# Three weight pieces on another DMA queue, their conversions re-placed, 42 filler products, and four hand-written lists rewritten in a DeltaNet + MLP kernel

## The chip, the core and the metric

The kernel runs on one core of a Trainium2 chip. The metric is the device time of one execution in microseconds (us), as the median of several runs. Engines are named as in the profile: PE (TensorE's matrix products; PEld is its loading of the stationary operand), DVE (VectorE), ACT (ScalarE), POOL (GpSimd), SP (SyncE, which here only issues DMAs). "The clock" is the share of TensorE's full clock that the chip granted.

## What is computed

All tensors are fp32 on the device; the two weight matrices arrive as 64-bit floats and are read as pairs of 32-bit words.

```python
# attention part: q, k, v are (4, 8, 768, 48), beta is (4, 8, 768)
k_n = k / (norm(k, axis=-1) + 1e-6)
state = 0
for t in range(768):
    y[:, :, t] = einsum('bhd,bhde->bhe', q[:, :, t], state)
    v_old = einsum('bhde,bhd->bhe', state, k_n[:, :, t])
    state = state + beta[:, :, t] * einsum('bhd,bhe->bhde', k_n[:, :, t], v[:, :, t] - v_old)
x = y.transpose(0, 2, 1, 3).reshape(4, 768, 384)
# MLP part: w_ch1 (384, 1536), w_ch2 (1536, 384)
mu, var = mean(x, -1), mean((x - mu) ** 2, -1)
xn = (x - mu) / sqrt(var + 1e-6) * g_ln
out = x + maximum(xn @ w_ch1, 0) @ w_ch2
```

## The kernel before

**Tiling.** The 768 time steps are cut into 12 chunks of 64. Two chunks form a slab. A chunk holds all 32 pairs of batch and head, so one chunk is 256 tokens of the MLP. The recurrence inside a chunk is turned into matrix form: a Gram matrix of the keys (`gram`, "G"), the inverse of a unit triangular matrix made from it, the masked product of keys and queries (`product`, "PT"), and then `recur`, in seven steps: the products with the state ("KQ", line 640, followed on DVE by line 645), the solved values u ("U", lines 651 and 655), the state's update ("S", lines 663 and 666), the chunk's output y ("PU", lines 671 and 676), and the layer norm ("L1" lines 682 to 685, "L2" lines 687 to 690, "N" lines 698 and 699).

**The inverse.** It is worked out on DVE by columns, 31 columns of two instructions (lines 543 and 548) for a slab; a generator yields after each second column, so "one step" is four such DVE instructions. In front of the steps stand "ga" (a clearing multiplication on ACT, line 522, which needs the tile xb of the inverse before to be free, and the turning of the Gram matrices on DVE, line 460), "sq" (a square root on ACT, line 527) and "no" (DVE, lines 529 to 537). Behind them stand "own" (line 466, two transposes), "xt" (lines 451 and 455) and "xn" (line 559). A block of 32 is inverted this way, and `join` ("J", three pieces) puts two blocks together by products on PE (p_e, line 568; p_z, line 614), scaled copies on ACT (line 581) and copies on DVE and ACT (line 619). A prime at a name means the slab of the current chunk, no prime means the next slab. The first slab has blocks of 16 (`first_blocks`) and one more joining stage, `first_join` (lines 598 to 607).

**The MLP.** "H" is one of 12 hidden pieces: six PE instructions (line 732) and a ReLU on ACT (line 736), in two PSUM banks used by turns, so an H can start only when the ReLU of the H two before it has run. The second product is done with seven products of half size, P1 to P7 (line 787, twelve PE instructions each), sums of their operands on DVE, S1 to S4 and the four "T" that are made once (line 716), and seven result sums d1 to d7 (all in line 792). The first chunk's MLP (`ffn`) has the plain form.

**The weights.** They come in 12 pieces of 768 KB ("words", three buffers). `to_fp32` turns one piece into fp32 in five steps: one on ACT (line 300), four on DVE (lines 302, 304, 308 and 313). The next piece can be fetched when a buffer is free.

**Order.** There are three stretches. In the first (lines 836 to 909) the program's order is kept on every engine and queue (`in_this_order`): it prepares chunks 0 and 1 and carries chunk 0 through `recur`, with `keep_warm` products on a tile of zeros in between. In the second (lines 934 to 953) a `Plan` gives each piece a due time, and the tile framework sets the order. The third (lines 959 to 1041) goes by "slots", again with the order kept on every engine: slot c does `recur` of chunk c and the MLP of chunk c - 1, in the order of a list of names. Slots 2 to 5 have lists of their own in `orders`; slots 6 and on take `even` and `odd` by turns. Whatever a list doesn't name with "r" is done at "R": `left` counts the steps. TK and TQ turn the loaded keys and queries on DVE (line 336), Vk is the keys' norm (three squares on ACT, line 402 and 404, two sums on DVE, line 408, a root on ACT) and Vs scales v by it (line 418).

Of the kernel before, what the change touches and what calls it, by code (L numbers as in the profile page):

```python
# [82 lines left out]
def kernel(  # L83
# [127 lines left out]
    def fetch_words(eng=nc.gpsimd):  # L211
        if len(words) < len(pieces):
            src = pieces[len(words)][1]
            words.append(early_pool.tile([128, WN, 2], U32, name="words", bufs=3))
            out_ = words[-1].rearrange("p n w -> p (n w)")
# [338 lines left out]
    def join(chunks, both=()):  # L554
# [6 lines left out]
        for c, xn in zip(chunks, xns):  # L561
# [12 lines left out]
            for e in range(2):  # L574
                r1 = slice(e * C + BK, (e + 1) * C)
                if both and e:
                    for _ in both:
                        pass
                    nc.vector.tensor_scalar_mul(es[r1], p_e[r1], -1.0)
                else:  # L580
                    nc.scalar.mul(es[r1], p_e[r1], -1.0)  # L581
# [236 lines left out]
    NW = len(pieces)  # L818

# [16 lines left out]
    with in_this_order(tc) as last:  # L836
        grams_01 = []
        keep_warm(3)
        for c in two:
# [3 lines left out]
            next(grams_01[c])  # L843
        inv = first_blocks(two)
        for _ in range(3):
# [3 lines left out]
        for _ in range(3):  # L849
            fetch_words(nc.scalar)  # L850
# [3 lines left out]
        nc.vector.tensor_scalar_mul(scale_w[:, 1, 0:KC], g_sb, 2.0**-52)  # L854
        for i in range(FB // 2):
            next(inv)
            if i == 4:
                keep_warm(4, mark=True)
        knrm = norm_parts(0, xts[NXT - 1])
        next(knrm)  # L860
        joining = first_join(0)
        next(joining)
        keep_warm(1, 4)
        turned(0, 1)
        knrm = next(knrm)
        scale_v(0, knrm)
        piece = to_fp32(0)
        for _ in range(3):
            next(piece)
# [4 lines left out]
        joining = join((0,), both=piece)  # L874
        next(joining)
        next(joining)
        keep_warm(1)
        piece = to_fp32(1)
        next(piece)
# [5 lines left out]
        fetch_words()  # L885
# [12 lines left out]
        for _ in piece:  # L898
            pass
        fetch_words()  # L900
        piece = to_fp32(2)
        next(piece)
        for i in range(4):
            next(recur_0)
            if i == 1:
                keep_warm(4)
        for _ in piece:
# [40 lines left out]
    plan.spread(inverses[1], 3 + BK // 4, 24, 38, whole=False)  # L948
# [3 lines left out]
    with behind(tc, after):  # L952
# [7 lines left out]
        2: """O H H H H H H H H R' own' H KQ xt' xn' H J' T T T T H H J' P1 S1 U J' S2 d1 P2 d2 S S4 PU  # L960
            TK(a2) P6 d6 S3 L1 G(a2) P5 d5 TK(b2) L2 P7 d7 N G(b2) TQ(b) P3 d3 PT(b) P4 d4
            ga sq no Vk Vs""",
        3: """KQ H r H r H r H r U TQ(a2) H r H r H r S H r H r H H H PU P1 L1 S1 S2 d1 PT(a2) P2
# [108 lines left out]
```

## Time and profile before

| | |
|---|---|
| median of 13 runs | 577.27 us (573.87 to 581.63) |
| the profiled execution | 576.48 us, of which the span from the first to the last instruction is 574.6 us |
| busy share of the span | PE 92%, PEld 79%, DVE 69%, ACT 30%, POOL 3% |
| mean granted clock | 0.958 |
| first stretch | about 0 to 57 us |
| second stretch | about 57 to 120 us |
| start of KQ in slots 2 to 7 | 134.39, 174.11, 216.45, 259.40, 307.60, 345.57 us |

A timeline row gives the start in us, the duration in us, the engine, the line, the operation, the tile written and those read, the shapes (for PE rows x columns of the stationary operand, then out), and how many like instructions were merged. In brackets stand the engine's idle time before it and what ended it; "issue" means that nothing the profile shows was waited for. A window row gives, for each engine, the busy time and the number of instructions, then the granted clock, the DMA engines' busy share and GB/s. PE's fp32 products appear as two instructions each, and each of these as one weight load and one product.

### The profile page before, as it was taken

The numbers are of one execution on the slowest core, as the hardware profiler recorded it, in microseconds if no ns is written. First come the engines' busy times: TensorE is split into PE (matmuls) and PEld (weight loads), VectorE is DVE, ScalarE is ACT, GpSimd is POOL, SyncE is SP. The second block draws the span as 40 slices with busy tenths as digits, with TensorE's granted clock in tenths as the row PEclk, the third lists the DMA queues.
The fourth block names the chain that finished last, engine by engine and source line by source line (L and its number), as shares of the span: only waits on it lengthen the run. The fifth ranks groups of instructions, "written<-read, shape, count | busy, mean of one in ns | idle before, by whom it ended". The sixth has DMA issues, their size and how long they took to land.

```text
span 574.6 us, 20506 instructions
## 1 busy us (share of the span) xinstructions
PE 528.1 (92%) x9298; PEld 451.2 (79%) x9298; DVE 394.3 (69%) x815; ACT 173.2 (30%) x352; POOL 15.3 (3%) x36
## 2 busy tenths in 40 slices
PE   5389896987998999999999999999999999999996
PEld 2155675566887898798888898888898988988996
DVE  5866987999568998499974899736899540523212
ACT  1233344311353224512225322255222232222120
POOL 6000110000000000000000000000000000000000
PEclk9577997989899999999989999999999999999999
DMA  4646987760046235024324204203212010010101
GB/s 59 140 152 130 193 202 186 118 110 1 3 62 108 29 42 101 5 29 84 47 33 93 30 1 86 29 14 74 30 35 51 2 31 2 1 30 1 29 0 29
DMA packets 158390, 34.47 MB, mean 60 GB/s; under 512 B 153680, under 2 KB 156768, under 8 KB 158304
## 3 DMA queue, kind: packets, MB, share of 16 engines
q1 hardware_dynamic: 143776, 22.27, 24.0%
q0 software_dynamic: 1456, 7.10, 3.7%
q10 hardware_dynamic: 13072, 3.80, 2.9%
q8 instruction: 73, 1.20, 0.8%
q14 instruction: 13, 0.11, 0.1%
HBM read 28.43 MB, written 4.72 MB: 58 GB/s over the span
## 4 chain that ended last, share of the span: by engine, by line
PE 59%; DVE 16%; issue 12%; DMA 5%; ACT 4%; ACTq 2%; POOL 1%; SPq 0%; DVEq 0%; POOLq 0%
PE p_h L732 25%; PE p_a L787 12%; PE p_o L787 9%; DVE xb L548 3%; DVE tmp L543 3%; DMA words<-in_moe_w_ch_dram 2%; PE p_u L651 2%; PE p_e L568 2%; PE p_g L358 1%; DMA tb<-in_k_dram 1%; PE p_z L614 1%; PE p_g L383 1%; PE p_k L640 1%; PE p_s L663 1%; PE p_y L671 1%
## 5 line engine op out<-in xcount | busy, mean ns | idle before, releaser
L732 PE MATMUL p_h<-xnt,w_sb 128*128 128x256 f32 x864 | 201.5, 389 | 5.6 <-ACT h L736 2.6
L732 PEld LDWEIGHTS p_h<-xnt,w_sb 128*128 128x128 f32 x864 | 163.5, 193 | 30.8 <-ACT h L736 3.5
L736 ACT ACTIVATE h<-p_h 128x256 f32<-128x256 f32 x144 | 55.0, 383 | 154.7 <-PE p_h L732 147.9
L548 DVE TENSOR_TENSOR xb<-xb,tmp 128x31 f32<-128x31 f32 (+20 forms) x170 | 56.9, 335 | 5.7
L543 DVE TENSOR_TENSOR tmp<-xb,gb 128x31 f32<-128x31 f32 (+15 forms) x155 | 52.6, 339 | 4.2
L787 PE MATMUL p_o<-w_sb,h 128*128 128x192 f32 x264 | 48.0, 332 | 0.0
L787 PE MATMUL p_a<-t,h 128*128 128x192 f32 x264 | 47.0, 328 | 0.0
L787 PEld LDWEIGHTS p_o<-w_sb,h 128*128 128x128 f32 x264 | 42.7, 190 | 0.9
L787 PEld LDWEIGHTS p_a<-t,h 128*128 128x128 f32 x264 | 42.8, 190 | 0.3
L682 DVE BATCH_NORM_STATS2 st<-x_ln 128x6 f32<-128x384 f32 x24 | 12.9, 542 | 34.6 <-ACT x_ln L676 34.5
L830 PE MATMUL p_w<-zeros 128*64 128x512 f32 (+1 forms) x30 | 21.5, 862 | 14.0 <-DVE zeros L827 10.8
L787 PE MATMUL p_a<-t,s 128*128 128x192 f32 x132 | 25.2, 343 | 2.9 <-DVE o L792 2.8
L787 PEld LDWEIGHTS p_a<-t,s 128*128 128x128 f32 x132 | 23.1, 201 | 3.8 <-DVE o L792 3.7
L699 ACT COPY xnt<-p_n 128x384 f32<-128x384 f32 x24 | 10.4, 482 | 51.0 <-PE p_n L698 51.0
L619 DVE COPY xt<-p_z 32x512 f32<-32x512 f32 x12 | 8.1, 678 | 23.7 <-PE p_z L614 23.7
L787 PE MATMUL p_a<-w_sb,h 128*128 128x192 f32 x132 | 24.3, 334 | 0.0
L787 PE MATMUL p_o<-w_sb,s 128*128 128x192 f32 x132 | 23.6, 328 | 0.0
L830 PEld LDWEIGHTS p_w<-zeros 128*64 128x64 f32 x30 | 4.9, 187 | 22.3 <-DVE zeros L827 10.9
L787 PEld LDWEIGHTS p_o<-w_sb,s 128*128 128x128 f32 x132 | 21.6, 190 | 0.1
L787 PEld LDWEIGHTS p_a<-w_sb,h 128*128 128x128 f32 x132 | 21.2, 190 | 0.6
L358 PEld LDWEIGHTS p_g<-kt 48*64 48x64 f32 (+1 forms) x896 | 13.9, 132 | 9.6 <-issue 4.5
L581 ACT ACTIVATE es<-p_e 32x512 f32<-32x512 f32 x23 | 13.5, 589 | 25.8 <-PE p_e L568 25.5
(123 smaller groups left out, 691.3 us busy)
## 6 DMA issues: line engine op xcount, KB each, us to landing
words<-in_moe_w_ch_dram POOLq DMA_DIRECT2D x9, 768.0 KB, 5.9
out_dram<-o SPq DMA_DIRECT2D x48, 96.0 KB, 2.8
k<-in_k_dram SPq DMA_DIRECT2D x44, 96.0 KB, 3.0
v_raw<-in_v_dram SPq DMA_DIRECT2D x22, 192.0 KB, 4.3
tb<-in_k_dram SPq DMA_DIRECT2D x48, 64.0 KB, 2.5
tb<-in_q_dram SPq DMA_DIRECT2D x44, 64.0 KB, 2.8
words<-in_moe_w_ch_dram ACTq DMA_DIRECT2D x3, 768.0 KB, 7.3
tb<-in_q_dram SPq DMA_DIRECT2D x44, 32.0 KB, 2.8
```

Of the source, the lines that this page charges most:

```text
L358: nc.tensor.matmul(out_, kt[rows, i, r0 : r0 + (BK if fine else C)], kt[rows, i, r0:C])
L543: nc.vector.tensor_tensor(out=t, in0=xb[:, :, 0:n, j : j + 1].to_broadcast([128, nb, n, w]), in1=gb[:, :, j : j + 1, j + 1 : L].to_broadca ...
L548: nc.vector.tensor_tensor(out=rest, in0=rest, in1=t, op=ALU.subtract)
L568: nc.tensor.matmul(p_e[r1, h], gsb[r0, h, BK:C], xn[r0, h])
L581: nc.scalar.mul(es[r1], p_e[r1], -1.0)
L651: nc.tensor.matmul(p_u[half(e ^ hp), hp, j], xt[half(e), 2 * j + hp], vv[half(e), 2 * j + hp])
L682: nc.vector.bn_stats(out=st[:, g], in_=y[:, g])
L699: nc.scalar.copy(xnts[c][:, :, g * 128 : (g + 1) * 128], p_n)
L732: nc.tensor.matmul(p_h, w1_sb[:, t, f * 128 : (f + 1) * 128], xnt[:, t], start=(t == 0), stop=(t == KC - 1),)
L736: nc.scalar.activation(h[f // HF][:, f % HF], p_h, ACTF.Relu)
L787: nc.tensor.matmul(p[n], a[:, f], b[:, f], start=(first and f == 0), stop=(f == HF - 1), skip_group_check=True,)
L830: nc.tensor.matmul(p_w[0:64, 0:width], zeros, zeros[:, None, :].to_broadcast([128, width, 64]), start=True, stop=True,)
```

## The change

In the first stretch:

- The first three weight pieces are no longer issued from ACT's queue behind the loads of q, k and v of chunk 0, but from SP's queue, at three places of the inverse of the first slab. A DVE memset of one element of the buffer holds each back until DVE is there.
- 42 `keep_warm` products of 64 columns are put on PE behind the two Gram matrices; the one of 256 columns behind `first_join`'s first half goes.
- The steps of the conversions of pieces 0, 1 and 2 are put at other places of the first chunk's chain, and `scale_v` of chunk 0 is moved behind the scaled copies of `join`.

In the second stretch six steps of the inverse of slab 1 are planned instead of eight, due two units earlier; the other two fall to slot 2. In the third stretch the lists of slots 2 to 5 are rewritten; `even` and `odd` stay.

```diff
-    def fetch_words(eng=nc.gpsimd):
+    def fetch_words(eng=nc.gpsimd, held=False):
...
+            if held:
+                nc.vector.memset(words[-1][0:1, 0:1, 0].bitcast(FP32), 0.0)
...
-    def join(chunks, both=()):
+    def join(chunks, both=False):
...
                 if both and e:
-                    for _ in both:
-                        pass
                     nc.vector.tensor_scalar_mul(es[r1], p_e[r1], -1.0)
...
+    EARLY = 6
...
+        keep_warm(42, 1)
         inv = first_blocks(two)
-        for _ in range(3):
+        next(inv)
+        fetch_words(nc.sync, held=True)
+        for _ in range(2):
             next(inv)
         load_blocks(q, 0, 1, (nc.scalar,))
         load_kv(0, nc.scalar)
-        for _ in range(3):
-            fetch_words(nc.scalar)
         for gen in grams_01:
             next(gen, None)
...
+        knrm = norm_parts(0, xts[NXT - 1])
+        next(knrm)
+        parts = [to_fp32(i) for i in range(3)]
+        next(parts[0])
         for i in range(FB // 2):
             next(inv)
+            if i in (1, 4):
+                fetch_words(nc.sync, held=True)
             if i == 4:
                 keep_warm(4, mark=True)
-        knrm = norm_parts(0, xts[NXT - 1])
-        next(knrm)
         joining = first_join(0)
         next(joining)
-        keep_warm(1, 4)
+        next(parts[0])
         turned(0, 1)
+        next(parts[0])
         knrm = next(knrm)
-        scale_v(0, knrm)
-        piece = to_fp32(0)
-        for _ in range(3):
-            next(piece)
+        next(parts[1])
+        next(parts[0])
         next(joining)
         masking = product(0)
         next(masking)
         to_xt(0)
-        joining = join((0,), both=piece)
+        joining = join((0,), both=True)
         next(joining)
+        next(parts[0], None)
+        fetch_words()
         next(joining)
+        next(parts[2])
+        scale_v(0, knrm)
         keep_warm(1)
-        piece = to_fp32(1)
-        next(piece)
...
         keep_warm(1)
-        fetch_words()
...
         next(recur_0)
         next(recur_0)
         keep_warm(1)
-        for _ in piece:
-            pass
+        for _ in range(3):
+            next(parts[1])
+        next(recur_0)
+        next(parts[1], None)
         fetch_words()
-        piece = to_fp32(2)
-        next(piece)
-        for i in range(4):
-            next(recur_0)
-            if i == 1:
-                keep_warm(4)
-        for _ in piece:
+        next(recur_0)
+        keep_warm(4)
+        next(recur_0)
+        next(parts[2])
+        next(recur_0)
+        for _ in parts[2]:
             pass
         fetch_words()
...
-    plan.spread(inverses[1], 3 + BK // 4, 24, 38, whole=False)
+    plan.spread(inverses[1], 3 + EARLY, 24, 36, whole=False)
...
-        2: """O H H H H H H H H R' own' H KQ xt' xn' H J' T T T T H H J' P1 S1 U J' S2 d1 P2 d2 S S4 PU
-            TK(a2) P6 d6 S3 L1 G(a2) P5 d5 TK(b2) L2 P7 d7 N G(b2) TQ(b) P3 d3 PT(b) P4 d4
-            ga sq no Vk Vs""",
-        3: """KQ H r H r H r H r U TQ(a2) H r H r H r S H r H r H H H PU P1 L1 S1 S2 d1 PT(a2) P2
-            d2 L2 S4 P6 d6 S3 TK(a4) P5 d5 r N r P7 d7 G(a4) TK(b4) P3 d3 r G(b4) P4
-            d4 r Vk Vs""",
-        4: """KQ H H R' own' H H H xt' xn' H H H J' H J' U H J' ga S H TQ(b) H sq no PU P1 L1 S1
-            S2 d1 PT(b) P2 d2 L2 S4 P6 d6 S3 r P5 d5 r N r P7 d7 r P3 d3 r P4 d4 Vk
-            Vs""",
-        5: """KQ H r H r H r H r U r H r H r H r TQ(a2) S H R H H TK(a4) H own H PU P1 L1 S1 S2 d1
-            PT(a2) P2 d2 L2 S4 P6 xt d6 S3 P5 d5 xn N TK(b4) P7 d7 J G(a4) P3 d3 J
-            G(b4) P4 d4 J Vk Vs""",
+        2: """O H H H H H H H H H H H R' own' KQ H xt' xn' P1 J' T T d1 P2 S1 T J' T d2 S2 U J' S4
+            S PU P6 d6 S3 L1 TK(a2) P5 d5 L2 G(a2) TK(b2) P7 d7 N G(b2) Vk TQ(b) P3 d3 PT(b) P4
+            d4 Vs ga""",
+        3: """KQ H H sq H no H r H r U TQ(a2) H r H r H r S H r H r H H PU P1 L1 S1 S2 d1 PT(a2)
+            P2 d2 L2 S4 P6 d6 S3 TK(a4) P5 d5 r N r P7 d7 G(a4) TK(b4) P3 d3 r G(b4) P4 d4 r
+            Vk Vs""",
+        4: """KQ H H R' own' H H H xt' xn' ga H H sq H J' no H J' r U H J' r S H r TQ(b) H r PU P1
+            L1 S1 S2 d1 PT(b) P2 d2 L2 S4 P6 d6 S3 r P5 d5 r N r P7 d7 r P3 d3 r P4 d4 Vk Vs""",
+        5: """KQ H r H r H r H r H R U TQ(a2) H H own TK(a4) H S H H xt H xn H PU P1 L1 S1 S2 d1
+            PT(a2) P2 d2 L2 S4 P6 d6 S3 TK(b4) J P5 d5 G(a4) N P7 d7 J P3 d3 G(b4) J P4 d4
+            Vk Vs""",
...
-    left[1] -= BK // 4
+    left[1] -= EARLY
```

## The prediction

> **What bounds the kernel now.** I read the page first, then windows cut at the three stretches and the slots, then the timeline around each gap of PE.
>
> ```profile
> PE   5389896987998999999999999999999999999996
> ...
> PEclk9577997989899999999989999999999999999999
> ...
> q8 instruction: 73, 1.20, 0.8%
> ```
> ```profile
> 0.00:57.00 57.00, 37.72 (x933) 20.11 (x933) 38.25 (x90) 15.91 (x27) 9.78 (x28) 0.76 0.54 120
> 57.00:120.88 63.88, 53.20 (x1086) 38.49 (x1087) 56.71 (x98) 24.06 (x44) 5.49 (x8) 0.95 0.82 167
> 120.88:345.57 224.69, 213.36 (x3882) 189.85 (x3883) 179.12 (x383) 72.28 (x147) 0.00 (x0) 0.97 0.29 47
> 345.57:574.60 229.03, 223.82 (x3399) 202.72 (x3398) 120.19 (x247) 60.99 (x134) 0.00 (x0) 1.00 0.14 28
> ```
>
> The columns are the stretch, its length, busy us of PE, PEld, DVE, ACT and POOL, the clock, DMA share and GB/s. Before 57 us neither engine is full: a chain of handshakes for chunk 0. From 57 to 120.88 DVE is busy 56.7 of 63.9 us, so it sets the pace, and a shift of its start goes through to the end. In slots 2 to 6 PE has 11.3 us of idle, behind them almost none. The rewritten lists can win no more than these 11.3 us and what the half clock in them costs.
>
> **The first chunk.** This is the stall that the fillers answer to:
>
> ```profile
> 30.05 1.26 PE L598 MATMUL p_e<-x_n,gsb 32*32 32x16 f32 x128
> ...
> 31.90 0.83 PE L606 MATMUL p_z<-own,es 32*32 32x16 f32 x78
> ...
> 35.25 0.60 PE L606 MATMUL p_z<-own,es 32*32 32x16 f32 x50 [2.52 <-issue]
> ...
> 35.90 0.42 DVE L607 TENSOR_TENSOR own<-own,p_z 128x256 f32<-128x256 f32 x1 [1.99 <-PE p_z L606]
> ```
>
> PE stops in the middle of one matrix product and waits for nothing that is seen. Counting PE's pairs (load and product) from the start, the gap at 11.23 comes after 223 pairs, this one after 478: 255 apart. The next, 0.32 us at 38.28, comes 127 pairs on. The instruction queue's packets are 1.20 MB / 73 = 16 KB. So PE's instructions come in blocks of about 128 pairs, and while one runs, one is fetched; from 35.25 to 38.60 that took 3.35 us, from about 30.7 (within L598) to 35.25 it took 4.5 with the DMA engines loaded by the words.
>
> The 42 fillers are 84 pairs, and 2 pairs go: all later block ends fall 82 pairs earlier in the program. One then lies in the four marked warm products at 24 us, the next 2 or 3 pairs before the end of L598 (about 31.4), the next 3 pairs before the end of L606. L598 has its block in time; the one for L606's end is there at 31.4 + 3.35 to 4.5 = 34.75 to 35.9. p_z ended at 35.85, so the gain is 0 to 1.1; I take 1.0, as the words are off the DMA engines by then. The 0.32 at 38.28 goes too: 1.3.
>
> The Trainium skill, "Runtime: NRT & Kernel Launch", section "Instruction fetch mechanics", speaks against this: it calls the crossing of a 16 KiB boundary mostly hidden. By it the fillers would bring nothing and the sum would end 1.3 higher; the 2.52 us here says that short products do not hide it.
>
> Other costs of this stretch:
> - Fillers: two 256-column products take 0.65 us at 31.24, started 0.27 apart, so 64 columns take 0.07 each, at half clock (the eight 512-column ones at 24.03, 0.85 apart) 0.11. 84 x 0.11 = 9 us from 13.2, done by 22.3; PE idles until 24.02, which hides them. Bounds: 1 us in all (by L598, 10 ns each) to 84 x 0.23 = 19 us (each as long as a weight load there); that would end at 32.6 and hold L598 up by some 9 us.
> - Three held memsets at 0.06 us (the row of L827) on DVE's path: +0.2.
> - The words leave ACT's queue (three issues, 24.25 to 25.98), so ACT's copies L370 start 1.7 earlier; SP has nothing queued from 6.5 to 45.85. Nobody waits for that: L598 is held by the warm products. Started at about 16, 19.5 and 23, the pieces share the DMA engines with k (landed 25.3; its squares could run at 26.6) and q (21.6; used at 29). The squares and one conversion step (1.6 + 0.9) stand before es at 31.4, so k may be 3 us late for nothing.
> - DVE's conversion steps: L302 and L304 stay under p_e and p_z; L308 comes before L607 and L313 behind L559, both under PE's work. Piece 1's last step (1.02) goes behind L666, where x_ln comes 0.7 later: +0.3. One step of piece 2 (0.55) fits a 0.36 gap: +0.2, and the tail behind it is 0.55 shorter. Together nothing. POOL's fetch of piece 4 gets some 2.5 us earlier, that of piece 5 some 2.5 later; its first use on DVE at 64.67 is 9 us after landing, so that is hidden.
>
> The stretch gives -1.1, bounds +0.5 to -4 (if the half clock from 35.82 to 49.47 went, another 3).
>
> **Slot 2.** PE waits for x_n at 137.97 and then pays half clock until 148.46:
>
> ```profile
> 141.94 1.92 PE L568 MATMUL p_e<-x_n,gsb 32*32 32x32 f32 x64 [3.97 <-DVE x_n L559]
> ```
> ```profile
> 141.63:148.46 6.83, 6.52 (x75) 5.56 (x76) 6.16 (x6) 1.56 (x3) 0.00 (x0) 0.50 0.01 2
> 288.40:291.82 3.42, 3.13 (x10) 3.13 (x11) 3.38 (x8) 0.00 (x0) 0.00 (x0) 0.50 0.13 16
> ```
>
> DVE's work up to x_n is the same (two steps of the inverse change place). With H, H and P1 (1.3 + 1.3 + 2.0) in the gap PE gets to J' at 142.5 without idling: 4.0 and about 3.3 of half clock are saved. But the list moves the waits. DVE then does T T d1 S1 T (2.7 + 0.4 + 0.9 + 1.4) before it copies p_z (L619, 0.7; ACT 0.6): U starts at 149.2, PE stands from 147.0, 2.2 us. TK(a2) is now behind S3 and L1 and ends at 159.7, P5 ends at 157.6: 2.1 us before G. Vk is in front of TQ(b): G(b2) ends at 164.9, ACT copies it (2.2), squares (1.6), DVE sums (0.5) and turns q (1.2), so PT(b) starts at 170.4, while P3 ended at 166.8: 3.6 us. PT and P4 (1.2 + 2.1) bring KQ of chunk 3 to 173.7 against 174.11: -0.4. J' U J' S PU now run with only P2 among them, 5.7 us of short products for six blocks of instructions: +1.0 of fetch stalls (0 to 2.8).
>
> After four of the six drops the clock stayed low for 6.83 us or more; a gap like this 3.6 (the ones above 2.1 us all did) costs 1.7 to 3.3; I take 2.5. Slot 2: +3.1.
>
> **Slot 3.** PE's 1.81 us at 178.98 come from ACT, which sits on "sq" and the squares of Vk; both are now past or behind two H. -1.8.
>
> **Slot 4.** Here the timeline of DVE counts:
>
> ```profile
> 220.26 0.95 DVE L645 TENSOR_TENSOR v_raw<-v_raw,p_k 128x768 f32<-128x768 f32 x1
> ...
> 223.99 2.08 DVE L466 STREAM_TRANSPOSE own<-xb 128x1024 f32<-128x1024 f32 x1
> ...
> 227.57 1.29 DVE L559 STREAM_TRANSPOSE x_n<-xt 128x512 f32<-128x512 f32 x2
> ```
>
> KQ began at 216.45, PE's eight H end at 229.09, x_n at 228.9: they meet. Slot 3's old list has 13 "r", the new one 11, so R' does four steps and not two, 3.0 us more (the two at 213.09 and 216.58 took 1.55 and 1.42), and the step before L645 is a bigger one (+0.3). "own" then ends 12.9 after KQ (9.6 + 3.3). "ga" is now among the H: its ACT part L522 (1.05) needs xb free, that is "own", and the ReLUs stand behind it, so the eighth H waits for its bank until 14.5 and ends at 15.8; then J' and H to 18.3; "sq" waits for the turning behind x_n (15.7 + 2.0), es ends at 19.6; J' to 20.9, copies 1.3, U at 22.3. Before, U began at 234.31, 17.9 after KQ. +4.4, and with 3.1, 1.3 and 1.4 us of idle so close together the clock again: 2.5. Slot 4: +6.9.
>
> **Slot 5.** The steps done in slot 4 relieve it, and the list becomes nearly `odd`. Slot 5 took 48.20, slot 7, which runs `odd`, 44.07: -4.1.
>
> ```profile
> 259.40:307.60 48.20, 45.26 (x931) 40.64 (x931) 37.89 (x81) 14.85 (x29) 0.00 (x0) 0.96 0.35 56
> ...
> 345.57:389.64 44.07, 43.86 (x931) 39.09 (x930) 29.68 (x60) 15.73 (x31) 0.00 (x0) 1.00 0.24 43
> ```
>
> **Sum.** -1.1 + 3.1 - 1.8 + 6.9 - 4.1 = +3.0 on 576.48, that is 579.5. The profiled execution is 0.8 below the median of the runs, so the forecast is 580.3: slower.
>
> **Rivals.**
> - The lists pay: slot 4's chain keeps up. Place: R' of slot 4; price: 6.9. It decides at the end of "own": if that is within 10 us of KQ and not 13, PE doesn't stop, and the sum is -3.9: 573.4, faster. For it: the gaps saved are seen, those added are worked out. Against it: d4, r, Vk, Vs and L645 follow each other on DVE behind PE's last product of slot 3, so nothing lets DVE start sooner. Chance 0.23.
> - Nothing changes: the half clock is added in one of slots 2 and 4 alone (-2.5, 577.8), or the front gains its 3 us of clock (577.3). For it: the clock's steps fall on a grid that takes no notice of the kernel's. Against it: every gap above 2.1 us was followed by a drop. Chance 0.18.
> - The filler doesn't do what it says: the block of L606 still comes late, or the fillers overrun 24 us. 581.6, up to 589. PE's count speaks for the place, the idle 10.8 us against the overrun. Chance 0.07.
>
> The forecast itself has 0.52. A measurement of this kernel tells about 0.3%, 1.7 us, from no change. Faster by more: the first rival and a little, 0.25; within: 0.16; slower: the forecast and the third, 0.59. For the range the low end takes in most of the first rival with the front's bound, 571; the high end adds the upper prices of the clock (0.8 twice), the fetch (1.8) and some of the third: 587. The forecast's own range is 577.5 to 586.
>
> **What would show it.** PE's gap in L606 short and three pairs before its end; the warm products still at 24 us; PE gaps before U, G and PT(b) in slot 2 and at the eighth H of slot 4, with the clock at 0.50 behind them; no gap of 1.8 in slot 3; slot 5 near 44 us. It is wrong if slot 4 takes less than 45 us, or if x_n of slot 2 comes more than 3 us before 141 us.

## The result, and the profile after

The changed kernel takes 584.17 us (median of 11 runs, 580.57 to 587.14) against 577.3: ratio 1.0112, 95% interval 1.009 to 1.0134. It is slower by 1.1%, about 6.9 us. The forecast was 580.3, slower by 3.0: the right side, inside the range, and less than half of the size. The profiled execution took 584.45 us with a span of 582.6, 8.0 more than the span before.

The page of the changed kernel, PE's busy tenths and granted clock in 40 slices, and the queue that fetches instructions:

```profile
PE   6759796888887999799999999999999999999997
...
PEclk9766999899788999899999999999999999999999
...
q8 instruction: 73, 1.20, 0.8%
```

PE is busier at the beginning (the fillers, second slice 7 instead of 3), which is no gain; the granted clock of slices 2 to 4 is 7, 6, 6 where it was 5, 7, 7. How many packets of instructions are fetched hasn't changed. Where the 8 us lie is seen from the times between the starts of KQ, and from J' of slot 2, the first PE work that waits for x_n:

| stretch | before | after | difference | forecast |
|---|---|---|---|---|
| start to J' of slot 2 (the front, carried on by DVE) | 141.94 | 145.62 | +3.7 | -1.1 |
| J' of slot 2 to KQ of chunk 3 | 32.17 | 37.86 | +5.7 | +3.1 |
| slot 3 | 42.34 | 40.26 | -2.1 | -1.8 |
| slot 4 | 42.95 | 48.50 | +5.5 | +6.9 |
| slot 5 | 48.20 | 44.14 | -4.1 | -4.1 |
| slot 6 | 37.97 | 37.17 | -0.8 | 0 |

From slot 7 on nothing differs. (The new list of slot 2 puts more PE work ahead of J', which PE does while it waits for x_n, so the first and second row are read together.) In these two executions the forecasts of the lists add up to +4.1 and they came to +4.3; the front is 4.8 us off. One execution doesn't fix the first row: three runs below with the front of before and the same work up to J' had J' at 141.3 to 144.1 us, and two with the new lists on the front of before had it at 143.40 and 143.60. The new front with the old lists had it at 145.87. So the front does cost here, but its 3.7 us are good to 1 or 2 at best.

**The front after.** The timeline of PE in the changed kernel, as the rows of L598 and L606 shown before:

```profile
25.05 5.34 PE L831 MATMUL p_w<-zeros 128*64 128x512 f32 x8 [3.45 <-DVE zeros L828]
```
```profile
30.35 1.22 PE L598 MATMUL p_e<-x_n,gsb 32*32 32x16 f32 x125
34.74 0.29 PE L598 MATMUL p_e<-x_n,gsb 32*32 32x16 f32 x3 [3.16 <-issue]
35.91 1.89 PE L606 MATMUL p_z<-own,es 32*32 32x16 f32 x124 [0.89 <-ACT es L601]
39.89 0.29 PE L606 MATMUL p_z<-own,es 32*32 32x16 f32 x4 [2.08 <-issue]
```

The block ends are where the fillers were to put them, three pairs before the end of L598 and four before the end of L606. But PE now stops at both, for 3.16 and 2.08 us, and the last pairs of L606 run until 40.18 (before 35.85). The transfers show one reason why the first block was late: busy tenths of the DMA engines from 26 to 34 us, 0.2 us for each digit, and the two queues that were busy from 28.2 to 32.5 us (packets, MB, and the time of their packets as a share of the 16 engines').

```profile
DMA  9994985997899999999999999999999992000001
```
```profile
q10 hardware_dynamic: 3531, 0.66, 104.4%
q1 hardware_dynamic: 53, 0.23, 13.6%
```

The block end before these lies in the warm products (eight instructions for the four that are marked) and is crossed by the sixth of them at 28.2 us. The fetch that follows starts at 32.51, 4.3 us later, when the engines fall idle, and PE goes on 2.2 us behind it. What fills the engines at that time is for the most part not the words (SP's queue, q1) but the many small packets of k and v, which ACT's queue (q10) sends late. Only at 34.73 is the next block end crossed; the fetch after it starts at 37.50, and so L606 stops as well. That second delay, 2.8 us with idle DMA engines, shows that their load isn't the only thing that makes a fetch late.

ACT has its own delay. Its timeline in the changed kernel:

```profile
30.48 2.34 ACT L372 COPY gsb<-p_g 32x512 f32<-32x512 f32 x4 [13.34 <-DMA k<-in_k_dram]
...
35.38 0.38 ACT L601 ACTIVATE es<-p_e 128x256 f32<-128x256 f32 x1
```

The forecast had these copies start 1.7 us sooner than 26.02, since the words leave ACT's queue. They start 4.5 later: ACT issues q, k and v from 16.90 to 30.44, 13.5 us where it took 8.3 before, because the words have already been put on the DMA engines. es at 35.38 is as late by ACT as by PE's stop at 34.74. That matters for the experiments: taking away one of the two leaves the other.

**The slots after,** as the windows shown before (the columns are the stretch, its length, busy PE, PEld, DVE, ACT, POOL, clock, DMA share, GB/s):

```profile
145.62:183.48 37.86, 29.91 (x718) 27.89 (x718) 21.18 (x31) 13.32 (x22) 0.00 (x0) 0.82 0.24 31
183.48:223.74 40.26, 39.90 (x676) 35.71 (x675) 33.27 (x73) 11.88 (x25) 0.00 (x0) 1.00 0.36 58
223.74:272.24 48.50, 43.42 (x803) 38.12 (x803) 41.05 (x96) 15.07 (x32) 0.00 (x0) 0.96 0.23 40
272.24:316.38 44.14, 43.93 (x932) 39.16 (x931) 32.04 (x66) 15.77 (x31) 0.00 (x0) 1.00 0.38 61
```

Slots 3 and 5 run at full clock with almost no idle, as forecast. The waits foreseen in slot 2 are there too, in PE's timeline:

```profile
145.62 1.20 PE L570 MATMUL p_e<-x_n,gsb 32*32 32x32 f32 x64 [1.76 <-DVE x_n L561]
...
151.83 0.31 PE L651 MATMUL p_u<-v_raw,xt 64*64 64x48 f32 x2 [1.65 <-DVE xt L619]
```
```profile
166.13 1.97 PE L360 MATMUL p_g<-kt 48*64 48x64 f32 x64 [2.14 <-DVE kt L338]
...
178.56 0.65 PE L385 MATMUL p_g<-qt,kt 48*64 48x64 f32 x29 [3.65 <-ACT xb L524]
```

They were forecast as 2.2 (U), 2.1 (G) and 3.6 (PT(b)); the first row's 1.76 is what is left of the 3.97 that the new order of PE was to fill. The releaser named in the last row is "ga" (L524), which ended at 178.46; what really comes late before it is ACT's and DVE's work of Vk: the copy of the Gram matrix, then squares until 176.7, the sums and only then the turning of q, to 178.4. Slot 4 went by the sketch of the forecast as well, which had the eighth H wait until 14.5 us after KQ for ACT's part of ga; it starts 14.31 after it:

```profile
238.05 2.93 PE L732 MATMUL p_h<-xnt,w_sb 128*128 128x256 f32 x6 [2.97 <-ACT h L736]
```
```profile
236.67 1.06 ACT L524 ACTIVATE xb<-eps 128x1024 f32<-128x1024 f32 x1 [3.76 <-DVE own L468]
237.63 0.64 ACT L736 ACTIVATE h<-p_h 128x256 f32<-128x256 f32 x2
```

ACT sits on L524 until "own" is there, and the ReLU (L736) that would free the bank stands behind it.

### The profile page after: what moved, and what is told of

Same layout as the page of the kernel before. It is cut to its first block, busy times and chain, and to the rows that moved or that the text cites. A ratio compares the mean times of both kernels' runs of the same rounds, so it can differ in the third digit from the quotient of the medians.

```text
span 582.6 us, 20671 instructions
## 1 busy us (share of the span) xinstructions
PE 534.3 (92%) x9380; PEld 460.4 (79%) x9380; DVE 393.8 (68%) x818; ACT 173.3 (30%) x352; POOL 15.6 (3%) x36
## 4 chain that ended last, share of the span: by engine, by line
PE 64%; DVE 13%; issue 13%; ACT 4%; DMA 3%; POOL 1%; SPq 0%; POOLq 0%; DVEq 0%; ACTq 0%
PE p_h L732 26%; PE p_a L787 13%; PE p_o L787 8%; DVE tmp L545 3%; DVE xb L550 3%; DMA words<-in_moe_w_ch_dram 2%; PE p_g L360 2%; PE p_u L651 2%; PE p_y L671 2%; PE p_s L663 2%; PE p_z L614 2%; PE p_g L385 2%; PE p_k L640 1%; PE p_y L640 1%; PE p_e L570 1%
## 5 line engine op out<-in xcount | busy, mean ns | idle before, releaser
L732 PE MATMUL p_h<-xnt,w_sb 128*128 128x256 f32 x864 | 198.5, 386 | 6.2 <-ACT h L736 4.0
L732 PEld LDWEIGHTS p_h<-xnt,w_sb 128*128 128x128 f32 x864 | 161.6, 191 | 30.4 <-ACT h L736 5.0
L736 ACT ACTIVATE h<-p_h 128x256 f32<-128x256 f32 x144 | 55.0, 383 | 156.0 <-PE p_h L732 149.1
L787 PE MATMUL p_a<-t,h 128*128 128x192 f32 x264 | 49.7, 340 | 1.0 <-DVE o L792 1.0
L787 PEld LDWEIGHTS p_a<-t,h 128*128 128x128 f32 x264 | 45.0, 198 | 1.7 <-DVE o L792 1.3
L831 PE MATMUL p_w<-zeros 128*64 128x64 f32 (+1 forms) x112 | 27.8, 425 | 6.6 <-DVE zeros L828 3.4
L360 PEld LDWEIGHTS p_g<-kt 48*64 48x64 f32 (+1 forms) x896 | 14.7, 140 | 16.4 <-issue 6.1
L360 PE MATMUL p_g<-kt 48*64 48x64 f32 (+2 forms) x896 | 16.5, 236 | 12.0 <-ACT gsb L375 4.4
L787 PE MATMUL p_a<-t,s 128*128 128x192 f32 x132 | 23.4, 327 | 0.6 <-DVE o L792 0.4
L699 ACT COPY xnt<-p_n 128x384 f32<-128x384 f32 x24 | 10.3, 482 | 43.7 <-PE p_n L698 43.7
L831 PEld LDWEIGHTS p_w<-zeros 128*64 128x64 f32 x112 | 11.8, 189 | 14.2 <-issue 7.1
L792 DVE TENSOR_TENSOR o<-p_a,x_ln 128x192 f32<-128x192 f32 x33 | 11.6, 352 | 16.9 <-PE p_a L787 16.9
L787 PEld LDWEIGHTS p_a<-t,s 128*128 128x128 f32 x132 | 21.6, 190 | 1.0 <-DVE o L792 0.7
```

The lines of the kernel that those rows point to most:

```text
L360: nc.tensor.matmul(out_, kt[rows, i, r0 : r0 + (BK if fine else C)], kt[rows, i, r0:C])
L732: nc.tensor.matmul(p_h, w1_sb[:, t, f * 128 : (f + 1) * 128], xnt[:, t], start=(t == 0), stop=(t == KC - 1),)
L736: nc.scalar.activation(h[f // HF][:, f % HF], p_h, ACTF.Relu)
L787: nc.tensor.matmul(p[n], a[:, f], b[:, f], start=(first and f == 0), stop=(f == HF - 1), skip_group_check=True,)
L831: nc.tensor.matmul(p_w[0:64, 0:width], zeros, zeros[:, None, :].to_broadcast([128, width, 64]), start=True, stop=True,)
```

## The experiments

A ratio is always to the kernel before, run on the same chip. "L606's end" counts from the start of L598, which takes out that the whole front can lie 1 to 2 us sooner or later from one execution to the next: 5.8 us before, 9.8 after. In the seven runs below whose front is that of the kernel before it lay between 6.3 and 7.1, so 5.8 is the low end, and values up to 7.1 are no loss that can be told.

### The front, one part at a time

The most direct one puts the fillers alone into the kernel before:

```diff
+        keep_warm(42, 1)
         inv = first_blocks(two)
```

> The kernel before with the 42 filler products and nothing else of the change. The prediction's step (block ends 3 pairs before the ends of L598 and L606, L606's block there in time): L606 ends about 1 us sooner and the time falls by about 1. Theory F (the fetch starts only when the words are off the DMA engines, so the earlier block end brings a gap of 2.5 to 4.5 us before the last pairs of L598 and then one of about 2 before the last of L606): from the start of L598 to the end of L606 9.5 to 10.5 us in place of 5.8, KQ of chunk 1 2 to 3.5 us later against the start of L598, time +1.5 to +3.5.

Measured: 582.59 us, ratio 1.0078 (1.0047 to 1.011). L606's end 10.15. PE's timeline of this kernel:

```profile
29.05 1.23 PE L598 MATMUL p_e<-x_n,gsb 32*32 32x16 f32 x125
34.63 0.28 PE L598 MATMUL p_e<-x_n,gsb 32*32 32x16 f32 x3 [4.36 <-issue]
34.85 1.11 PE L830 MATMUL p_w<-zeros 128*64 128x256 f32 x2
35.89 1.88 PE L606 MATMUL p_z<-own,es 32*32 32x16 f32 x122
38.91 0.30 PE L606 MATMUL p_z<-own,es 32*32 32x16 f32 x6 [1.13 <-issue]
```

Words and conversions are as before here and the stop in L598 is even longer. The fillers by themselves cost about 0.8%. Their step of the forecast falls. Of the 7.6 us that this execution's span is longer, 3.2 lie ahead of J' of slot 2 (145.18); it also took 4.4 longer in slots 4 and 5 with the old lists (44.58 and 50.98 us, before 42.95 and 48.20, at clocks of 0.96 and 0.93). That later block ends do all of this isn't shown, since another run with the fillers and the old lists (below) took 42.79 and 48.97. But all three runs with the fillers and the old lists stop in L358 (L360) of slot 5 for nothing that is seen, for 1.62, 1.45 and 1.40 us, and the kernel before doesn't. This kernel's:

```profile
310.00 0.97 PE L358 MATMUL p_g<-kt 48*64 48x64 f32 x45 [1.62 <-issue]
```

Then the words' new queue alone, at the three places of the change, on the kernel before:

```diff
-        for _ in range(3):
-            fetch_words(nc.scalar)
...
+        fetch_words(nc.sync, held=True)
```

> The kernel before with the first three words transfers held on SP's queue, as in the change, and nothing else of it. The prediction's step: ACT's copies start 1.7 us sooner and nobody waits, time the same. Theory W: ACT's own transfers wait behind the words, its copies start near 30 and es of L601 comes near 34 to 35, the fetch for L606 in time (words landed by 30); L606 ends 6.3 to 7 us after the start of L598 (5.8), time 0 to +1.5.

Measured: 578.74, ratio 1.0016 (0.9984 to 1.0047): not told from no change. Its ACT timeline:

```profile
29.55 2.34 ACT L372 COPY gsb<-p_g 32x512 f32<-32x512 f32 x4 [13.66 <-DMA k<-in_k_dram]
...
33.55 0.38 ACT L603 ACTIVATE es<-p_e 128x256 f32<-128x256 f32 x1
```

ACT is late by 3.5 us (4.5 in the changed kernel). But L606, which waits for es, then runs through without a stop and ends 5.8 after L598's start, as before: the fetch for L606 starts 1.5 us after its block end (2.1 in the kernel before), and the wait for es has taken the place of the wait for instructions. So the mechanism was wrong in the forecast and its price of nothing right.

The conversions alone are what is left with the front of the change, no fillers, the words on ACT's queue, and the lists of before.

> The changed kernel's front without the fillers and with the words on ACT's queue, and the four lists of before: only the new places of the conversion steps are left of the change. If these cost nothing, as the prediction has it, the time is within 0.3% of before and KQ of chunk 1 within 1.5 us of 80.8; if they hold DVE up ahead of L607 (x_n of chunk 0 came 8.8 us after L598 began in the run with neither, 7.5 before), 578.5 to 580 against 577.3.

Measured: 578.91, ratio 1.0026 (1.0003 to 1.0049). The profiled execution shows no loss: KQ of chunk 1 50.96 us after L598's start, before 50.72. At most a few tenths of a per cent.

The next three undo parts of the front in the changed kernel, with the new lists in it. First without the fillers:

```diff
-        keep_warm(42, 1)
```

> The changed kernel without the 42 filler products; words still on SP's queue. Two theories for the 3.6 us by which chunk 1's KQ is late (84.38 against 80.77). Theory F, the fillers: they put one block end 3 pairs before the end of L598 and one 4 pairs before the end of L606, where the fetch of the next block is late (gaps of 3.16 and 2.08 us). Without them the block ends lie as before, product L606 ends near 35.9 us (40.2 with fillers), KQ of chunk 1 is near 81 and the time about 580.5. Theory W, the words on SP's queue: they hold up ACT's own transfers (its copies L372 begin at 30.48, before at 26.02), so es of L601 comes at 35.4 to 35.8 whatever PE does, L606 ends at 37.7 or later and the time stays at 582 to 584.

Measured: 585.91, ratio 1.0112 (1.0067 to 1.0156): nothing gained that can be told, though both stops are gone and L606 ends at 6.6. This kernel's timelines of PE and DVE show other waits in their place:

```profile
30.14 1.26 PE L598 MATMUL p_e<-x_n,gsb 32*32 32x16 f32 x128
35.15 1.61 PE L606 MATMUL p_z<-own,es 32*32 32x16 f32 x128 [3.76 <-ACT es L601]
```
```profile
37.63 1.01 DVE L310 SCALAR_TENSOR_TENSOR words<-words,scale_w 128x768 f32<-128x768 uint32 x1
38.55 0.41 DVE L607 TENSOR_TENSOR own<-own,p_z 128x256 f32<-128x256 f32 x1
```

p_z ends at 36.77, and DVE takes it up at 38.55: its queue still holds the turning of q and conversion steps, which waited for ACT's late work. Both theories had a part of it: F for the stops, W for es at 35. But by KQ of chunk 1 this execution lay no further back than the new lists alone on the front of before (both 51.7 us after L598's start), so these waits don't account for its time, and what does isn't shown.

With the fillers, but the words back on ACT's queue behind v:

> The changed kernel with the three words transfers back on ACT's queue behind v, fillers kept. Theory W: ACT's copies start near 26 us again and the front is as before: KQ of chunk 1 near 81, time about 580.5. Theory F: the gap three pairs before the end of L598 stays, since the block's fetch still starts only when the words are off the DMA engines (32 to 33 us), es not before 35, a second gap before the end of L606, which ends at 38 to 40; KQ of chunk 1 at 83 to 84, time 582.5 to 584.

Measured: 584.92, ratio 1.0104 (1.0068 to 1.0141). ACT's copies start at 25.32, and PE still stops for 4.26 and 1.82; L606 ends at 10.3. Theory F, as expected of it.

Neither fillers nor words on SP's queue:

> The changed kernel without the fillers and with the words back on ACT's queue; what is left of the front is the new place of the conversions. If fillers and words are the whole of it, KQ of chunk 1 is at 80 to 81.5 and the time 579.5 to 581 (584.2 less 3.6 to 4.5). If the moved conversions on DVE and ACT cost something, KQ of chunk 1 stays above 82 and the time above 582.

Measured: 583.2, ratio 1.0076 (1.0043 to 1.011), L606's end 7.0. By its numbers it is the second case of the expectation: KQ of chunk 1 came at 84.95. But these numbers don't tell the two cases apart. PE stopped for 3.24 us in L606, whose fetch began 3.3 us after its block end (2.1 before); the run with the new lists alone (below), whose front is that of before, has the same stop:

```profile
36.68 0.88 PE L606 MATMUL p_z<-own,es 32*32 32x16 f32 x50 [3.52 <-issue]
```

And KQ of chunk 1 came 54.3 us after L598's start here, 54.5 in the run with the lists of slots 4 and 5 alone. So no loss by the conversions is shown; by themselves they measured +0.26%. With the new lists alone at 1.0037 (below) the intervals overlap, and whether anything is left over isn't settled.

Is it the exact place of the block ends? Two fillers fewer put all later block ends four pairs later:

```diff
-        keep_warm(42, 1)
+        keep_warm(40, 1)
```

> The changed kernel with 40 filler products in place of 42: all later block ends four pairs (load and product) later, so just behind the last pair of L598 and of L606. If the place of the block ends makes the gaps, the gaps of 3.16 us (three pairs before the end of L598) and 2.08 us (four before the end of L606) go; L606 then waits for es of L601 (35.8) or for its own block (34.8) and ends 37.7 to 38.5 (40.2 before). ACT's late copies stay, DVE still has its conversions to do, so KQ of chunk 1 gains 0.5 to 2 and the time 0.5 to 2: 582 to 583.7. If the gaps stay where they were in the program's pairs, the count of pairs isn't what places them.

Measured: 585.93, ratio 1.009 (1.0053 to 1.0127). The gaps moved exactly as counted:

```profile
29.27 1.26 PE L598 MATMUL p_e<-x_n,gsb 32*32 32x16 f32 x128
34.69 1.90 PE L606 MATMUL p_z<-own,es 32*32 32x16 f32 x128 [4.17 <-ACT es L601]
38.54 1.99 PE L385 MATMUL p_g<-qt,kt 48*64 48x64 f32 x64 [1.94 <-issue]
```

L598 and L606 run through, L606 ends at 7.3, and the stop stands in front of the next product, L385. So the count of pairs is what places the stops (shown), but the time didn't gain what can be told: a stop put behind L606 still stands ahead of L385 and L570, and DVE, behind ACT's late words, still had its conversions to do (L607 at 37.89, for a p_z of 36.59).

Now the words at 10 to 13 us, when the DMA engines are idle, on the kernel before:

```diff
+        for _ in range(3):
+            fetch_words(nc.sync, held=True)
         inv = first_blocks(two)
...
-        for _ in range(3):
-            fetch_words(nc.scalar)
```

> The kernel before with the first three words transfers on SP's queue ahead of the first steps of the inverse (about 11 to 13 us), where the DMA engines are idle. If it is the words on the DMA engines at 25 to 33 us that hold up the fetch for L606, the fetch starts about 1.1 us after its block end and the gap in L606 shrinks from 2.5 to 1 to 1.6 us, provided that ACT's transfers are through by 28; time -0.5 to -1.5. If ACT's transfers are held up by the words as on SP's queue in the changed kernel, es is late and the time is the same or up to 1.5 longer.

Measured: 576.91, ratio 0.9974 (0.9946 to 1.0001). PE's timeline:

```profile
31.92 0.83 PE L608 MATMUL p_z<-own,es 32*32 32x16 f32 x78
33.90 0.60 PE L608 MATMUL p_z<-own,es 32*32 32x16 f32 x50 [1.14 <-issue]
```

The block end is at the same pair as before, the fetch starts 0.84 us after it (2.07 before) and the stop is 1.14 instead of 2.52. Of the eight runs with the front of before none had the fetch sooner than 2.07 us after this block end (2.07 to 3.3); in the two with the words early it is 0.84 and 0.9. So the words' transfers on the DMA engines are what makes this fetch late; ACT's own transfers were through in time. And the fillers on top of this:

> The kernel before with the words early on SP's queue and the 42 fillers. If it is the words on the DMA engines that spoil the fillers, the fetch of the block that starts in the warm products begins 0.8 to 1.5 us after its start and is there at 31.5 to 32.5: the gap before the last pairs of L598 shrinks from 4.4 (filler alone) to 0 to 1, L606 ends 5 to 7 us after the start of L598 (10.2 with the fillers alone, 4.4 with the words early alone), time within 0.3% of the run with the words early alone. If the fillers cost in any case, since block ends three and six pairs ahead of the ends of two products make two waits, L606 ends 8 us or more after it and the time is 0.5 to 0.8% above before.

Measured: 582.03, ratio 1.0067 (1.0038 to 1.0096).

```profile
30.65 1.23 PE L600 MATMUL p_e<-x_n,gsb 32*32 32x16 f32 x125
33.64 0.23 PE L600 MATMUL p_e<-x_n,gsb 32*32 32x16 f32 x3 [1.76 <-issue]
...
34.44 1.20 PE L608 MATMUL p_z<-own,es 32*32 32x16 f32 x122
38.14 0.30 PE L608 MATMUL p_z<-own,es 32*32 32x16 f32 x6 [2.50 <-issue]
...
308.54 0.92 PE L360 MATMUL p_g<-kt 48*64 48x64 f32 x45 [1.40 <-issue]
```

The DMA engines were idle, and still the fetch began 2.1 us after the block end in the warm products; the first stop shrinks from 4.36 to 1.76, not to the 0 to 1 expected, and the second is longer. The pairs of one block run in 1.2 to 1.9 us, and in the runs with the words early a block is there 3.2 to 4.7 after the start of the one before it, so two block ends shortly before the ends of two products mean two waits. Before, one of the two ends lay in the middle of L598, where PE had instructions left, and the other in L606. L606's (here L608's) end is at 7.8, and by the times the fillers cost as much as without the early words. But the two waits aren't where this execution lost its time: J' of slot 2 begins at 142.33, with the words early alone at 142.23, and it is slots 2, 4 and 5 that took longer, 33.96, 44.93 and 50.79 us against 32.04, 43.15 and 48.41. That the fillers cost is shown; that it is by the stops in the first stretch is shown for the stops and not for the time.

### The lists

The changed front with the four lists of before:

> The changed kernel's front with the four slot lists of before (and the plan's share of the inverse with them). Theory L, the lists cost 4.3 us by themselves (slot 2 +5.7, slot 3 -2.1, slot 4 +5.6, slot 5 -4.1, slot 6 -0.8): the time is about 580 and the slots after KQ of chunk 3 take 42.3, 43.0 and 48.2 as before, shifted by 3.6. Rival: the lists only pass on the front's delay and cost nothing: 583 to 584.

Measured: 581.65, ratio 1.0056 (1.0023 to 1.0089), nearer to Theory L: 1.0056 of 577.3 is 580.5. The other way round, the new lists on the front of before:

> The kernel before with the four new slot lists (and the plan's share of the inverse that goes with them), front untouched. Theory L: the lists cost 4.3 us by themselves, time 580 to 582, KQ of chunk 1 near 81, the slots 4 and 5 at 48 to 50.6 and 44.1. Rival (the lists pay when x_n of slot 2 isn't late; place: the gap of 1.76 us before J' and the half clock behind it): slot 2's J' starts at or before 142.5 without a gap and the time is 577 or less.

Measured: 582.09, ratio 1.0037 (1.0008 to 1.0065). The rival falls: a gap of 1.28 us before J' remains, and slots 4 and 5 take 50.32 and 44.07. So front and lists each cost by themselves, about 0.6% and 0.4%, and together 1.1%.

Slot 2: Vk is moved from ahead of TQ(b) to behind P4, nothing else.

```diff
-  N G(b2) Vk TQ(b) P3 d3 PT(b) P4 d4 Vs ga
+  N G(b2) TQ(b) P3 d3 PT(b) P4 d4 Vk Vs ga
```

> The kernel before with the four new lists, and in slot 2 Vk moved from ahead of TQ(b) to behind P4. If Vk on ACT's and DVE's queues is what PT(b) waits for (3.62 us before L383 at 173.44 in the run with the new lists alone), that gap goes, and some of the half clock behind it: KQ of chunk 3 comes 3 to 5.5 us sooner (177.5 to 180 from a J' at 143.4) and the time is 577 to 579.5. If PT(b) waits for q's own path, the gap stays above 2 and the time at 582.

Measured: 575.87, ratio 0.9977 (0.9947 to 1.0007), 0.6% below the new lists with Vk in front. J' to KQ of chunk 3, in the windows of the new lists alone and of this kernel:

```profile
143.40:183.05 39.65, 32.78 (x718) 30.52 (x719) 21.28 (x31) 13.32 (x22) 0.00 (x0) 0.74 0.25 32
```
```profile
143.60:173.43 29.83, 25.68 (x719) 23.52 (x719) 20.19 (x29) 12.16 (x20) 0.00 (x0) 0.94 0.20 27
```

The gap before PT(b) falls from 3.65 to 0.18, and the clock rises from 0.74 to 0.94: length times what the clock lacks of full speed is 10.3 us in the one and 1.8 in the other. But most of that half clock lies ahead of the gap, as the windows cut at it show (two of the new lists alone, up to the gap and behind it; one of this kernel, up to it):

```profile
143.40:173.44 30.04, 26.82 (x642) 24.99 (x642) 17.56 (x26) 10.47 (x17) 0.00 (x0) 0.77 0.18 24
177.09:183.05 5.96, 5.96 (x76) 5.50 (x77) 1.32 (x2) 0.00 (x0) 0.00 (x0) 0.51 0.52 68
```
```profile
143.60:170.01 26.41, 22.44 (x642) 20.57 (x642) 18.61 (x27) 10.47 (x17) 0.00 (x0) 0.94 0.14 20
```

Of the 9.8 us between the two, 3.6 lie ahead of the gap, 3.5 are the gap, and 2.7 lie behind it. So in these two the clock behind the stop cost somewhat less than the stop, and the first part is not the token's doing: the lists are the same up to there. The execution of the new lists alone is also the longest of its twelve. By the times the token is worth 0.6%, 3.5 us. G's stop of 2.14 us is there again in this kernel, and no half clock follows it.

Slot 4: the new lists of slots 4 and 5 alone, so that R' has two steps and not four.

> The kernel before with the new lists of slots 4 and 5 alone; slot 3 keeps its 13 steps r, so R' of slot 4 has two steps, as before, and not four. Theory R (the two steps more make own late): slot 4 takes 43 to 46 us, slot 5 44.1 and the time is 574 to 576. Theory G (ga among the H of slot 4: its ACT part waits for own and holds the ReLUs): slot 4 still takes 47 to 50, slot 5 44.1, time 577 to 580.

Measured: 576.83, ratio 0.9942 (0.9917 to 0.9966). Slot 4 takes 46.78 us, between the two theories, slot 5 44.07. The 2.97 us before the eighth H are gone and J' starts 12.57 after KQ as in the kernel before (17.17 after the change), with ga still among the H: ga holds up the ReLUs only if own is late, and the two steps more of R' make it late. If the place of ga costs something by itself, that shows in the next kernel, which puts it behind J':

```diff
-  4: KQ H H R' own' H H H xt' xn' ga H H sq H J' no H J' r U H J' r S H ...
+  4: KQ H H R' own' H H H xt' xn' H H H J' H J' ga U H J' sq no r S H ...
```

> As the run with the new lists of slots 4 and 5 alone, and in slot 4 ga, sq, no moved behind the second and third J' with one step r less. If ga is what holds the ReLUs, slot 4 takes 42.5 to 44 and slot 5 44.1, time 572.5 to 574; if the steps of R' alone are the cause, it takes what the run without this move takes, within 0.5.

Measured: 576.55, ratio 0.9941 (0.9912 to 0.997), slot 4 46.73: the same. It costs nothing that can be told here. What slot 4 still takes over the 42.95 of before goes with its "r" (five before, nine in the change, eight in this kernel), though no run changes these alone: PE waits for DVE, for the turned q and before sums of the second product (0.93, 1.27 and 0.89 us; the 0.78 before U was there before).

### What the experiments point to

Keep slots 4 and 5 as changed, R' short, and ACT's "sq" out of the way in slot 3:

```diff
-  2: ... P4 d4 ga sq no Vk Vs
+  2: ... P4 d4 Vk Vs ga
-  3: KQ H r H r H r H r U TQ(a2) H r H r H r S H r H r H H H PU ...
+  3: KQ H H sq H no H r H r U TQ(a2) H r H r H r S H r H r H r H r PU ...
```

> Slot 2 of before with ga alone behind Vk, Vs (sq and no go to slot 3), slot 3 of the changed kernel with two steps r more (13), slots 4 and 5 of the changed kernel. If sq and Vk on ACT are what PE's gap of 1.8 us in slot 3 is made of, slot 3 takes 40.2 to 41 and not 42.35, slot 4 stays at 46.8: 1.5 to 2 us less than the run with the lists of slots 4 and 5 alone, 574.5 to 575.5 (0.991 of before). Rival (the two steps r that are put back hold up DVE before P1): slot 3 at 42 and the time as in that run.

Measured: 575.28, ratio 0.9957 (0.9934 to 0.9979), slot 3 41.19. The 1.8 us stop of slot 3 is gone and the slot 1.2 us shorter; slot 4 took 50.07 in this execution, with half clock in it. By the times it is no gain that can be told over the lists of slots 4 and 5 alone (0.9942); 0.991 was expected.

Then the new beginning of slot 2 with fewer of the waits that the change put behind it:

```diff
+  2: O H H H H H H H H H H H R' own' KQ H xt' xn' P1 J' T P2 J' d1 S1 U T J' S2 d2 T S T S4
+     PU TK(a2) P6 d6 S3 L1 G(a2) P5 d5 TK(b2) L2 P7 d7 N G(b2) TQ(b) P3 d3 PT(b) P4 d4 Vk Vs ga
```

> As the run before it, with slot 2's new beginning (three H ahead of KQ, P1 ahead of J') and the rest of slot 2 as in the list of before: T spread one by one, TK(a2) ahead of P6, TQ(b) ahead of Vk. If the new beginning is worth its 4 us of idle and the half clock behind it, and the lists lost it only by the waits added behind it, KQ of chunk 3 comes 3 to 6 us earlier against J' than in the run before (J' to KQ 27 to 30 us where before takes 32.2) and the time is 570 to 572.5. If what is saved comes back as waits for DVE, it is 574 to 577.

Measured: 570.59, ratio 0.9883 (0.9846 to 0.9921). J' to KQ of chunk 3:

```profile
144.42:173.34 28.92, 24.47 (x720) 22.11 (x719) 19.48 (x29) 12.12 (x20) 0.00 (x0) 1.00 0.30 40
```

The idle before J' and all half clock behind it are gone. P1 now stands ahead of J', which shortens this stretch too: KQ of chunk 3 starts at 173.34, 0.8 us sooner than before, in an execution that is the longest of its six. By the times this is what the change's lists could have been worth. Two more on this base, ga, sq, no later in slot 4, and the words early:

> The fastest so far (new lists of slots 2 to 5 with slot 2's tail and slot 3's steps r put right) with slot 4's ga, sq, no behind the second and third J'. If the half clock of slot 4 (0.50 at 235 to 245 us in the one, 1.00 in the run with ga later) comes from J' H J' being thinned by them, slot 4 takes 46.7 in place of 49.9 in the profile and the time is 567.5 to 570.5 (0.984 of before); if it comes and goes by chance, the time is 570 to 571.5.

> The fastest so far (slots 2 to 5 put right, ga early in slot 4) with the three words transfers on SP's queue at 11 to 13 us. If the two gains add, 0.9883 and 0.9974 of before give 0.986, 568.5 to 570.5 us; if slot 2's x_n, which DVE sets, takes the front's gain away, 570 to 573, as without the words early.

Measured: 575.62, ratio 0.9942 (0.9912 to 0.9972) for the first, though its profile shows slot 4 at 46.55 and full clock. Its times fall into two groups, five of 571.0 to 572.9 us with a mean clock of 0.965 or more and seven of 575.4 to 577.5 with 0.964 or less; the profiled execution, 572.88, is of the first. So profile and times don't disagree; what lowers the clock in the seven isn't shown. The second: 570.21, ratio 0.9893 (0.9858 to 0.9929), in its profile L606 ends at 4.8 and KQ of chunk 1 at 78.95. Beside 0.9883 that is no further gain that can be told; both beat the kernel before by 1.1% and the changed one by 2%.

## Why the prediction was wrong

**The step that failed** is the front: "L598 has its block in time; the one for L606's end is there at 31.4 + 3.35 to 4.5 = 34.75 to 35.9", worth -1.1. The places were right to the pair. Wrong was when a block is asked for and how long it takes. The warm products that cross the block end begin at 25.05 and not at 24, the crossing is by the sixth of the eight, at 28.2, and the block was usable 6.5 us after it and not 3.35 to 4.5. The forecast took the words to be off the DMA engines by then; they nearly were, but k and v, held up by them, had taken their place. And it let L606's block be asked for at 31.4, which holds only if L598 isn't stopped; in fact it was asked for at 34.74. The fillers alone measured +0.78% (about 4.5 us) where they were to gain 1.3. The stops are seen; how much of the 4.5 us comes through them isn't settled, since with the words early the fillers cost as much without a later J'. The third rival, "the block of L606 still comes late", named this mechanism with a chance of 0.07, and its 581.6 to 589 is where the time lies. The rule that the working weighed (the Trainium skill, "Runtime: NRT & Kernel Launch", section "Instruction fetch mechanics": crossing a 16 KiB boundary is mostly hidden) spoke against the fillers, but would have had them change nothing; with short products on PE the runs show stops of 1.1 to 4.4 us at such ends.

**The words' queue:** the direction for ACT was wrong (4.5 us later, not 1.7 sooner), the price of nothing right within the interval. In the changed kernel it is a second, equal delay of es; undoing the fillers or the queue alone gave no gain that can be told (1.0112 and 1.0104).

**Conversions** at nothing: their run gave +0.26%, barely clear of zero.

**Slot 2:** the three waits were right to 0.6 us (1.65, 2.14, 3.65 against 2.2, 2.1, 3.6). Mis-sized was the half clock: 3.3 us were to be saved and 2.5 added. By length times the missing clock, the stretch from J' lost 3.2 us before (0.90 over 32.17) and 6.8 after (0.82 over 37.86): +3.6 and not -0.8. The wait for x_n, which was to be filled, stayed at 1.76, and at 1.28 with the front of before. And "every gap above 2.1 us was followed by a drop" holds in the profile of before and not beyond it: slot 5's old list stops PE for 2.4 us in seven profiles, with half clock at that place in four of them and none in three.

**Slots 3 and 5:** right to 0.3 us. **Slot 4:** the eighth H was put at 14.5 us after KQ and came at 14.31, U at 22.3 and came at 22.1; PE's idle time grew by 3.9 us and not 4.4, and the clock cost about 1.9 (0.96 over 48.50) and not 2.5. The rival that slot 4 keeps up fell: own did end late, and with two steps less in R' it didn't.

What stays open: what besides the load of the DMA engines makes a fetch late; by what way the fillers cost, beside the stops in the first stretch and in slot 5, where two runs with the fillers lost more in slots 4 and 5 and one didn't; what brings the half clock at one execution's stop and not at another's; and why slot 4's two forms measure the same on the kernel before (0.9942, 0.9941) and differ on the best lists (0.9883, 0.9942).

## What to carry to other kernels

Where an engine stops in the middle of a product for nothing that the profile shows, count its instructions between stops; but before block ends are moved, follow the whole chain for each block: what crosses the end before it, when that runs, and what the DMA engines carry at that moment. Take the load off the DMA engines first: here that shortened a stop, and shifted ends only exchanged one wait for another. In a hand-written order, look for what stands in each queue ahead of the short operation that the next product needs: here one token was worth 0.6%, and two steps made slot 4 some 1.7 us longer in single profiles (48.50 against 46.78).

## What the hardware showed that was not expected

- With the words on ACT's queue, the fetch of PE's instructions in L598 began 2.07 to 3.3 us after the block end in eight runs with the front of before, and 0.84 and 0.9 us after it in the two where the words had been moved out of the way. With the fillers it began 4.3 us (the changed kernel) and 4.7 us (the fillers alone) after the end in the warm products, and still 2.1 with the words early and the DMA engines idle.
- Transfers issued by another engine slow an engine's own issuing: ACT took 13.5 us in place of 8.3 to issue q, k and v when the words were on SP's queue ahead of them.
- Half clock comes at a stop of PE in one execution and not in another: at the same stop of 2.4 us in slot 5, four of seven profiles show it and three don't.
